# A fused attention and mixer kernel: conversions spread over the steps, v as two float16 parts, weight loads queued behind transposes, six scale factors in one product

## The chip, the cores and the metric

The program runs on one core of a Trainium2 chip. The core has TensorE (matmuls, PE in the profile), VectorE (DVE), ScalarE (ACT), GpSimd (POOL) and SyncE (SP, which issues the DMAs). The metric is device time in microseconds, the median over the executions that were timed.

## The reference

Causal attention with 4 batches, 12 heads, 448 positions and a head size of 64, then a token and channel mixer, then a layer in which a learned angle rotates the values:

```python
scores = q @ k.T / 8;  scores[mask] = -1e9;  attn = softmax(scores);  x = attn @ v      # 48 heads
h  = relu(x.T @ w_tok1) @ w_tok2;  u = x + h.T                  # over the positions
x2 = u + relu(u @ w_ch1) @ w_ch2                                # over 768 channels
th = x2 @ w_theta;  y = w_tok_r @ (x2*cos(th)) + w_tok_i @ (x2*sin(th));  u = x2 + y
out = u + relu(u @ w_ch)
```

The weights come as float64, q, k and v as float32.

## The kernel before

**Attention** runs over 24 pairs of heads (batch and pair of heads), each in 7 steps (the list `TILES`), so 168 steps, numbered through. A step takes one tile of scores: `scores` multiplies, reduces the row's maximum on VectorE (L338), takes the exponential on ScalarE (L340), and then hands the probabilities over in one of two ways. In pairs 0 to 11 (`NATPV`) TensorE transposes float32 probabilities (L347) and `pv` multiplies them with float32 v (L375). In pairs 12 to 23 the probabilities are split into two float16 parts `ph` (L157, L360), a transposing DMA on SP's queue makes `pt` of them (L363), and `pv` multiplies with v cut into three bfloat16 parts (L386): `prep` makes those parts with two subtractions on VectorE (L164, `v_mid`). `pv` of a step comes 4 steps (`LAG`) after its scores. `finish` divides by the row sums, and after each second pair `tokmix` does the first mixer.

**Units.** The channel mixer is 96 units of 18 matmuls of 128x448: for each batch and each half `fh`, 6 of `ch1_unit` (relu on ScalarE L459, float16 high part on POOL L160, low part on VectorE L461) and 6 of `ch2_unit` (its result is scaled with a factor `f` and added on VectorE, L473). `f` is one small product on POOL (L130) per unit. A unit's weights are float16 pairs `ws`, 384 KB, which `load_unit` streams from DRAM on SP's queue (L222). `UNIT_STEPS` says at which step each unit starts; the units that are left when attention ends run in a dense row, and behind them comes the third layer (from L657).

**Conversions.** The 24 tiles of `w_ch1` and `w_ch2` and four of `w_tok` are first made float32 from float64 in steps of their own: a load of 768 KB into `raw`, `abs64` on ScalarE (L173), three operations on VectorE (L180 to L182), squares on ScalarE (L124), a small matmul with `power`, which chooses a power of two `s`, then the high part on POOL (L160) and the low part on VectorE (L193, `ws`), and a store. The table `ROUNDINGS` sets their steps, one about every 3.4 steps from 14 to 92. Six tiles of `w_ch` are converted late.

**Before a batch's units**, `split_ready` calls `power` for the scale `s_u` and splits the six tiles `accs` into `ut` (high part ScalarE L157, low part VectorE L193). In `power` the products on POOL are `s` and `p`.

**Order.** A scheduler builds each engine's queue from the order of the code and priorities (`tc.high_priority`); `tc.issue_after(x)` puts what its block issues behind x on x's engine. Every engine and SP's queue take their instructions in order, so a waiting one holds those behind it. On-chip buffers are shared by tag: 8 of `ws`, 5 of `pt`, 4 of `f`, 3 of `ph` and `raw`, 4 PSUM banks for `ps_mm`.

Of the kernel before, what the change touches and what calls it, by code (L numbers as in the profile page):

```python
# [35 lines left out]
FIRST_UNIT, DENSE, RATE = 50, 88, (42, 29)  # L36
UNIT_STEPS = [FIRST_UNIT + n * (DENSE - FIRST_UNIT) // 14 if n < 14 else
              DENSE + -(-(n - 14) * RATE[0] // RATE[1]) for n in range(72)]
ROUNDINGS = [(at_step, n - 4) for n, at_step in enumerate((3, 4, 8, 9))] + [(14 + n * 78 // 23, n) for n in range(24)]
# [15 lines left out]
def fused(ctx, tc, q, k, v, w_tok1, w_tok2, w_ch1, w_ch2, w_theta, w_tok, w_ch, out):  # L55
# [76 lines left out]
    def power(p, s, sq):  # L132

        ps = mm_bank()
        n = sq.shape[-1]
        nc.tensor.matmul(ps[:, 0:1], lhsT=ones, rhs=tiny, start=True, stop=False)
        for j in range(n):
            nc.tensor.matmul(ps[:, 0:1], lhsT=ones, rhs=sq[:, j:j + 1], start=False, stop=j == n - 1)
        g = main.tile([P, 2], F32, tag="g", name="g", bufs=4)
        nc.vector.tensor_scalar(out=g[:, 0:1].bitcast(U32), in0=ps[:, 0:1].bitcast(U32), scalar1=1, scalar2=EXPONENT,  # L140
                                op0=ALU.logical_shift_right, op1=ALU.bitwise_and)
        two_over(g[:, 1:2], g[:, 0:1])
        product(s, g[:, 1:2], 2.0 ** -51, 1.0)
        product(p, g[:, 0:1], 2.0 ** 64, 1.0)
# [122 lines left out]
    def prep(b, pr):  # L267
# [28 lines left out]
        v1 = vr.bitcast(BF16).rearrange("p (n w) -> p n w", w=2)[:, :, 1]  # L296
        vm = ap2.tile([P, 9 * D], F32, tag="v_mid", name="v_mid", bufs=1)
        rest_to(pick("v"), vm, vr, v1)
        v2, v3 = (vm.bitcast(BF16).rearrange("p (n w) -> p n w", w=2)[:, :, z] for z in (1, 0))
        rest_to(pick("v"), v3, vm, v2)  # L300
        return qs, kh, kl, (v1, v2, v3)
# [3 lines left out]
    class Pair:  # L305
        def __init__(self, b, pr, parts):
            self.b, self.pr = b, pr
            self.qs, self.kh, self.kl, self.v = parts
# [57 lines left out]
    def pv(pp, i, h):  # L366
# [11 lines left out]
        if i == 0:  # L378
            jobs = [(0, c, 8) for c in range(3)] + [(1, c, 8) for c in range(2)]
        else:  # L380
            jobs = [(0, c, 6 + h) for c in range(3)]
            for u in range(i):
                jobs += [(1 + u, c, 2 * u + h) for c in range(3)]
                jobs += [(1 + i + u, c, 2 * u + h) for c in range(2)]
# [4 lines left out]
    def finish(pp, xb, xg):  # L389
        ps, sm = pp.ps, pp.sm  # L390
        nc.vector.tensor_scalar(out=sm[:, 0:7], in0=sm[:, 0:7], scalar1=1e-9, scalar2=1.0 if pp.native_pv else PSC, op0=ALU.add, op1=ALU.mult)
# [48 lines left out]
    ready = set()  # L440

# [25 lines left out]
    def ch2_unit(b, uT, acc, fh, d, w):  # L467
        ps = mm_bank()
        f = main.tile([P, 1], F32, tag="f", name="f", bufs=4)
        product(f, p_w2[:, fh * 6 + d:fh * 6 + d + 1], h_scale[0], 1.0)  # L470
# [15 lines left out]

    def load_unit(n):
        if n < len(units) and n not in loaded and (n >= 24 or n in stored):
            b, fh, c, t = units[n]
            loaded[n] = stream_tile(wd[f"c{c}", fh, t])  # L490
# [4 lines left out]
    def split_ready():  # L495

        b = halves[0]
        if b < B and None not in accs[b]:
            s = s_u[:, b:b + 1]
            power(p_u[:, b:b + 1], s, sq_u[b])  # L500
# [49 lines left out]
    def run_units(n):  # L550
        for _ in range(n):
# [11 lines left out]
            for ahead in range(LOOK + (u >= 24)):  # L563
                load_unit(at[0] + ahead)
# [35 lines left out]
    for n, (b, pr, t) in enumerate(steps):  # L600
        if t == 0:
            eng.update(ENGINES.get(b * NPR + pr, {}))
# [40 lines left out]
        run_units(sum(at_step == n for at_step in UNIT_STEPS))  # L643
    for n in range(len(steps) - LAG, len(steps)):
# [308 lines left out]
```

## Time and profile before

| | us |
|---|---|
| median of 3 runs | 905.37 (903.42 to 909.47) |
| profiled execution, its own time | 907.62 |
| its span, first to last instruction | 905.8 |
| busy: TensorE, VectorE, ScalarE, POOL | 868.4, 632.0, 538.1, 166.0 |
| granted TensorE clock, mean | 0.981 |

The span is 1.8 us shorter than the execution's own time. A busy TensorE is counted from modelled ends of pipelined matmuls. Step 56's scores are reduced at 121.4 us, step 84's at 210.4, step 126's at 330.2, and the last one's at 478.

### The profile page before, as it was taken

How to read it: one execution, taken by the hardware profiler on the slowest of the kernel's cores; microseconds unless marked ns; L12 is line 12 of the kernel's file. 1: busy time of each engine (PE TensorE's matmuls, PEld its weight loads, DVE VectorE, ACT ScalarE, POOL GpSimd, SP SyncE). 2: the span in 40 equal slices, each digit the busy share in tenths (PEclk: the TensorE clock that was granted, in tenths of full speed). 3: DMA queues.
4: the chain of work that ended last, by engine and by line, in shares of the span. 5: the costliest groups of instructions: out<-in, count | busy, mean ns of one | idle time of the engine just before them, and what ended most of it. 6: DMA issues, size and time to landing. Idle time of an engine off the chain costs nothing.

```text
span 905.8 us, 16756 instructions
## 1 busy us (share of the span) xinstructions
PE 868.4 (96%) x5979; PEld 563.7 (62%) x5979; DVE 632.0 (70%) x1499; ACT 538.1 (59%) x1247; POOL 166.0 (18%) x313
## 2 busy tenths in 40 slices
PE   7999699998988999899999998999999999999998
PEld 6888567776755667565666564556555555555554
DVE  7899867979997776738686328767875557566442
ACT  6788766767765654546573328546755457566441
POOL 3142322314141110101211102052211001101000
PEclk9999989999899999999999999999999999999999
DMA  7867745767799986747448568740440231231011
GB/s 225 243 194 237 281 166 194 259 210 202 211 279 319 261 204 140 202 110 193 142 103 224 162 195 298 258 131 10 145 143 29 86 114 39 92 114 45 21 57 72
DMA packets 105795, 149.67 MB, mean 165 GB/s; under 512 B 61104, under 2 KB 72304, under 8 KB 105712
## 3 DMA queue, kind: packets, MB, share of 16 engines
q1 hardware_dynamic: 105168, 147.59, 54.4%
q0 software_dynamic: 384, 0.79, 0.4%
q8 instruction: 47, 0.77, 0.4%
q14 instruction: 36, 0.29, 0.1%
q10 hardware_dynamic: 160, 0.23, 0.1%
HBM read 112.39 MB, written 22.81 MB: 149 GB/s over the span
## 4 chain that ended last, share of the span: by engine, by line
PE 74%; DVE 10%; DMA 8%; ACT 3%; issue 3%; POOL 1%; SPq 1%; DVEq 0%; ACTq 0%; POOLq 0%
PE ps_mm L228 17%; PE ps_mm L227 17%; PE ps_mm L229 17%; DMA pt<-ph 4%; PE ps_sc L229 3%; PE ps_sc L227 3%; PE ps_sc L228 3%; PE ps_pv L375 3%; PE ps_sc L331 2%; PE ps_pv L386 2%; PE ps_mm L347 2%; DVE sb L338 1%; PE ps_sc L333 1%; DVE wf L181 1%; DMA ws<-w_c 1%
## 5 line engine op out<-in xcount | busy, mean ns | idle before, releaser
L227 PE MATMUL ps_mm<-h,ws 128*128 128x448 f16 x432 | 152.8, 356 | 2.8 <-DMA ws<-w_c 2.8
L228 PE MATMUL ps_mm<-h,ws 128*128 128x448 f16 x432 | 153.4, 356 | 0.0
L229 PE MATMUL ps_mm<-h,ws 128*128 128x448 f16 x432 | 153.2, 356 | 0.0
L227 PEld LDWEIGHTS <-ws 128*128 128x128 f16 x720 | 71.1, 99 | 70.0 <-issue 5.7
L227 PE MATMUL ps_mm<-ut,ws 128*128 128x448 f16 x288 | 103.2, 359 | 8.8 <-ACT ut L157 8.2
L229 PEld LDWEIGHTS <-ws 128*128 128x128 f16 x720 | 71.1, 99 | 65.1 <-issue 5.2
L228 PEld LDWEIGHTS <-ws 128*128 128x128 f16 x720 | 71.1, 99 | 62.1 <-issue 4.9
L340 ACT ACTIVATE sb<-sb,mx 128x320 f32<-128x320 f32 (+3 forms) x168 | 89.3, 533 | 26.8 <-DVE mx L338 22.6
L228 PE MATMUL ps_mm<-ut,ws 128*128 128x448 f16 x288 | 103.0, 358 | 0.3 <-DVE ut L193 0.3
L229 PE MATMUL ps_mm<-ut,ws 128*128 128x448 f16 x288 | 102.8, 357 | 0.0
L338 DVE CUSTOM_DVE_ANT_0 sb<-ps_sc,mask 128x320 f32<-128x320 f32 (+3 forms) x168 | 73.8, 454 | 13.2 <-PE ps_mm L347 8.8
L124 ACT ACTIVATE junk<-acc 128x448 bf16<-128x448 f32 x72 | 41.2, 572 | 61.6 <-DVE acc L845 40.7
L375 PE MATMUL ps_pv<-v_raw,ptf 128*128 128x128 f32 (+1 forms) x456 | 63.2, 276 | 1.9 <-DVE x L398 1.7
L375 PEld LDWEIGHTS ps_pv<-v_raw,ptf 128*128 128x128 f32 x456 | 58.8, 191 | 6.9 <-ACT sb L340 1.9
L459 ACT ACTIVATE t<-ps_mm,c_scale 128x448 f32<-128x448 f32 x48 | 30.0, 628 | 54.5 <-PE ps_mm L229 45.9
L160 POOL TENSOR_SCALAR h<-t 128x448 f16<-128x448 f32 x48 | 31.3, 653 | 150.6 <-ACT t L459 150.3
L461 DVE TENSOR_TENSOR h<-t,h 128x448 f16<-128x448 f32 x48 | 31.3, 654 | 37.6 <-POOL h L160 37.5
L360 DVE SCALAR_TENSOR_TENSOR ph<-sb,ph 128x64 f16<-128x64 f32 (+3 forms) x156 | 43.0, 321 | 16.4 <-ACT ph L157 16.1
L157 ACT ACTIVATE ph<-sb 128x192 f16<-128x192 f32 (+3 forms) x84 | 36.5, 442 | 29.3 <-DMA pt<-ph 28.5
L130 POOL TENSOR_SCALAR f<-p_w,c_h 128x1 f32<-128x1 f32 x48 | 24.6, 516 | 145.2 <-DVE acc L473 129.0
L473 DVE SCALAR_TENSOR_TENSOR acc<-ps_mm,f,acc 128x448 f32<-128x448 f32 x48 | 32.4, 678 | 25.1 <-PE ps_mm L229 24.9
L227 PE MATMUL ps_sc<-th,ut 128*128 128x384 f16 x144 | 46.9, 326 | 0.0
(210 smaller groups left out, 2118.4 us busy)
## 6 DMA issues: line engine op xcount, KB each, us to landing
ws<-w_c SPq DMA_DIRECT2D x120, 384.0 KB, 4.0
raw<-in_w_ch_dram SPq DMA_DIRECT2D x30, 768.0 KB, 4.5
w_c<-ws SPq DMA_DIRECT2D x30, 384.0 KB, 3.8
q_raw<-in_q_dram SPq DMA_DIRECT2D x16, 448.0 KB, 3.6
k_raw<-in_k_dram SPq DMA_DIRECT2D x16, 448.0 KB, 5.6
v_raw<-in_v_dram SPq DMA_DIRECT2D x24, 288.0 KB, 3.4
x2d<-acc SPq DMA_DIRECT2D x24, 224.0 KB, 3.2
acc<-x2d SPq DMA_DIRECT2D x24, 224.0 KB, 2.9
```

The source lines that it names most:

```text
L124: nc.scalar.activation(j[:, 0:src.shape[-1]], src, AF.Square, accum_out=dst)
L157: nc.scalar.activation(dst, src, AF.Copy, scale=scale)
L160: e.tensor_scalar(out=dst, in0=src, scalar1=scale, scalar2=0.0, op0=ALU.mult, op1=ALU.add)
L227: nc.tensor.matmul(ps, lhsT=ka(a[:, 0]), rhs=kb(b[:, 0]), start=first, stop=False)
L228: nc.tensor.matmul(ps, lhsT=ka(a[:, 0]), rhs=kb(b[:, 1]), start=False, stop=False)
L229: return nc.tensor.matmul(ps, lhsT=ka(a[:, 1]), rhs=kb(b[:, 0]), start=False, stop=last)
L338: pp.first = nc.vector.tensor_tensor_reduce(out=dst, in0=src, in1=msk, op0=ALU.add, op1=ALU.min, scale=-0.125, scalar=3.0e38, accum_out=pp ...
L340: pp.last = nc.scalar.activation(sb[:, 0:kk], sb[:, 0:kk], AF.Exp, bias=pp.mx[:, j:j + 1], scale=-1.0, accum_out=pp.sm[:, j:j + 1])
L360: nc.vector.scalar_tensor_tensor(out=dst, in0=sb[:, c0:c1], scalar=PSC, in1=hi[:, c0:c1], op0=ALU.mult, op1=ALU.subtract)
L375: pp.pv = nc.tensor.matmul(pp.ps[:, reg:reg + n], lhsT=pt[:, u], rhs=pp.v[0][:, vt * D:vt * D + n], start=(u == 0), stop=(u == len(blks) - 1))
L461: gates[0] = nc.vector.tensor_tensor(out=t[:, 1], in0=f, in1=t[:, 0], op=ALU.subtract)
L473: nc.vector.scalar_tensor_tensor(out=acc[d], in0=ps[:, 0:S], scalar=f, in1=acc[d], op0=ALU.mult, op1=ALU.add)
```

## The change

Five things change. (1) `ROUNDINGS`: conversions stand 5 steps apart up to step 49, then 3.2 apart from 52 to 100. (2) `UNIT_STEPS`: the first unit starts at step 52 instead of 50, the first 12 stand 3 steps apart, 12 more 1.75 apart from step 88, and the dense rate of 29 units in 42 steps starts at 107 with the 24th. By the table 28 units have started by step 107 before, and 24 now. (3) v of pairs 12 to 23 is scaled by a power of two and cut into two float16 parts, `v_hi` on POOL (`copy_to("P", ...)`) and the rest on VectorE, written into `v_raw`; `pv` makes three products of each block of probabilities (high with both parts, low with the high one) instead of five. ScalarE squares v, and a small matmul and POOL's products `sv` choose the scale. (4) `load_unit` issues its DMA behind the latest transposing DMA of the current pair (`behind`), and always one unit further ahead. (5) From batch 1 on the six factors `f` of a half are one product `f6` of 128x6. `power` for `s_u` gets a high priority.

```diff
-FIRST_UNIT, DENSE, RATE = 50, 88, (42, 29)
-UNIT_STEPS = [FIRST_UNIT + n * (DENSE - FIRST_UNIT) // 14 if n < 14 else
-              DENSE + -(-(n - 14) * RATE[0] // RATE[1]) for n in range(72)]
-ROUNDINGS = [(at_step, n - 4) for n, at_step in enumerate((3, 4, 8, 9))] + [(14 + n * 78 // 23, n) for n in range(24)]
+FIRST_UNIT, DENSE, RATE = 52, 107, (42, 29)
+UNIT_STEPS = [FIRST_UNIT + 3 * n if n < 12 else 88 + (n - 12) * 7 // 4 if n < 24 else
+              DENSE + -(-(n - 23) * RATE[0] // RATE[1]) for n in range(72)]
+ROUNDINGS = [(at_step, n - 4) for n, at_step in enumerate((3, 4, 8, 9))]
+ROUNDINGS += [(14 + 5 * n if n < 8 else 52 + (n - 8) * 16 // 5, n) for n in range(24)]
...
-    def power(p, s, sq):
+    def power(p, s, sq, unit=None):
...
-        product(p, g[:, 0:1], 2.0 ** 64, 1.0)
+        if p is not None:
+            product(p, g[:, 0:1], 2.0 ** 64, 1.0)
+        if unit is not None:
+            product(unit, g[:, 1:2], 2.0 ** -51, PSC)
...
-        v1 = vr.bitcast(BF16).rearrange("p (n w) -> p n w", w=2)[:, :, 1]
-        vm = ap2.tile([P, 9 * D], F32, tag="v_mid", name="v_mid", bufs=1)
-        rest_to(pick("v"), vm, vr, v1)
-        v2, v3 = (vm.bitcast(BF16).rearrange("p (n w) -> p n w", w=2)[:, :, z] for z in (1, 0))
-        rest_to(pick("v"), v3, vm, v2)
-        return qs, kh, kl, (v1, v2, v3)
+        return qs, kh, kl, (vr,)
+
+    values = {}
+
+    def value_squares(n):
+        sq = main.tile([P, 1], BF16, tag="sqv", name="sqv", bufs=2)
+        squares(sq, parts[n][3][0])
+        values[n] = sq
+
+    def value_split(n):
+
+        vr = parts[n][3][0]
+        sc = main.tile([P, 2], F32, tag="sv", name="sv", bufs=3)
+        scale, unit = sc[:, 0:1], sc[:, 1:2]
+        power(None, scale, values.pop(n), unit)
+        hi = ap2.tile([P, 9 * D], F16, tag="v_hi", name="v_hi", bufs=2)
+        copy_to("P", hi, vr, scale)
+        lo = vr.bitcast(F16).rearrange("p (n w) -> p n w", w=2)[:, :, 0]
+        nc.vector.scalar_tensor_tensor(out=lo, in0=vr, scalar=scale, in1=hi, op0=ALU.mult, op1=ALU.subtract)
+        parts[n] = (*parts[n][:3], (hi, lo), unit)
...
-            jobs = [(0, c, 8) for c in range(3)] + [(1, c, 8) for c in range(2)]
+            jobs = [(0, 0, 8), (0, 1, 8), (1, 0, 8)]
         else:
-            jobs = [(0, c, 6 + h) for c in range(3)]
+            jobs = [(0, 0, 6 + h), (0, 1, 6 + h)]
             for u in range(i):
-                jobs += [(1 + u, c, 2 * u + h) for c in range(3)]
-                jobs += [(1 + i + u, c, 2 * u + h) for c in range(2)]
+                jobs += [(1 + u, 0, 2 * u + h), (1 + u, 1, 2 * u + h), (1 + i + u, 0, 2 * u + h)]
...
-        f = main.tile([P, 1], F32, tag="f", name="f", bufs=4)
-        product(f, p_w2[:, fh * 6 + d:fh * 6 + d + 1], h_scale[0], 1.0)
+        if b == 0:
+            f = main.tile([P, 1], F32, tag="f", name="f", bufs=4)
+            product(f, p_w2[:, fh * 6 + d:fh * 6 + d + 1], h_scale[0], 1.0)
+        else:
+            if d == 0:
+                f_six[0] = main.tile([P, DT], F32, tag="f6", name="f6", bufs=2)
+                product(f_six[0], p_w2[:, fh * 6:fh * 6 + 6], h_scale[0], 1.0)
+            f = f_six[0][:, d:d + 1]
...
+    behind = [ExitStack]
+
     def load_unit(n):
         if n < len(units) and n not in loaded and (n >= 24 or n in stored):
             b, fh, c, t = units[n]
-            loaded[n] = stream_tile(wd[f"c{c}", fh, t])
+            with behind[0]():
+                loaded[n] = stream_tile(wd[f"c{c}", fh, t])
...
-            power(p_u[:, b:b + 1], s, sq_u[b])
+            with tc.high_priority(AHEAD):
+                power(p_u[:, b:b + 1], s, sq_u[b])
...
-            for ahead in range(LOOK + (u >= 24)):
+            for ahead in range(LOOK + 1):
...
+        behind[0] = lambda pp=(b, pr): queued(pairs[pp])
...
+        nx = b * NPR + pr + 1
+        nxt = (nx // NPR, nx % NPR)
+        split_next = nx < B * NPR and nx not in NATPV
+        if t == 2 and split_next:
+            with tc.issue_after(pairs[b, pr].last.ins):
+                value_squares(nxt)
         if n >= LAG:
             with tc.high_priority(AHEAD):
                 late_step(n - LAG)
+            if t == 4 and split_next:
+                with tc.issue_after(pairs[steps[n - LAG][0:2]].pv.ins), tc.high_priority(AHEAD // 2):
+                    value_split(nxt)
```

The names at three places. On POOL, where the first units begin (`p_u` and `s_u` are `split_ready`'s products, `c_h` and `f` the units' factors, `ws` and `s` a conversion's), the queue before:

```order
L130 TENSOR_SCALAR p_u_148<-g_1407 128x1
L130 TENSOR_SCALAR c_h_1487<-p_fh_147,p_u_148 128x1
L130 TENSOR_SCALAR f_2083<-p_w2_143,c_h_1487 128x1
L130 TENSOR_SCALAR f_2169<-p_w2_143,c_h_1487 128x1
L130 TENSOR_SCALAR f_2249<-p_w2_143,c_h_1487 128x1
L130 TENSOR_SCALAR f_2408<-p_w2_143,c_h_1487 128x1
L130 TENSOR_SCALAR s_u_149<-g_1407 128x1
L130 TENSOR_SCALAR p_w2_143<-g_1476 128x1
L130 TENSOR_SCALAR s_1472<-g_1476 128x1
L160 TENSOR_SCALAR ws_1471<-wf_1364,s_1472 128x768
```

and the same place now:

```order
L131 TENSOR_SCALAR p_u_148<-g_1326 128x1
L131 TENSOR_SCALAR c_h_1456<-p_fh_147,p_u_148 128x1
L131 TENSOR_SCALAR f_2107<-p_w2_143,c_h_1456 128x1
L131 TENSOR_SCALAR s_u_149<-g_1326 128x1
L131 TENSOR_SCALAR p_w2_143<-g_1445 128x1
L131 TENSOR_SCALAR f_2203<-p_w2_143,c_h_1456 128x1
L131 TENSOR_SCALAR s_1441<-g_1445 128x1
L164 TENSOR_SCALAR ws_1440<-wf_1364,s_1441 128x768
```

`s_u`, for which the split of the first units' input waits, stood behind four products `f` and stands behind one.

On SP, from pair 14 to pair 15 (`ws` loads are a unit's weights, `w_c...<-ws` a conversion's store, `DMA_TRANSPOSE` the probabilities), the queue before:

```order
L363 DMA_TRANSPOSE pt<-ph 128x7x128
L363 DMA_TRANSPOSE pt<-ph 128x2x128
L363 DMA_TRANSPOSE pt<-ph 128x3x128
L476 DMA x2d_2_71<-acc 128x448
L222 DMA ws<-w_c_1_5_116 128x1536
L222 DMA ws<-w_c_0_0_93 128x1536
L222 DMA ws<-w_c_0_1_94 128x1536
L222 DMA ws<-w_c_0_2_95 128x1536
L476 DMA x2d_3_72<-acc 128x448
L222 DMA ws<-w_c_0_3_96 128x1536
L222 DMA ws<-w_c_0_4_97 128x1536
L222 DMA ws<-w_c_0_5_98 128x1536
```

and, at the transposes of the same sizes, now:

```order
L382 DMA_TRANSPOSE pt<-ph 128x7x128
L501 DMA x2d_0_69<-acc 128x448
L501 DMA x2d_1_70<-acc 128x448
L382 DMA_TRANSPOSE pt<-ph 128x2x128
L226 DMA ws<-w_c_1_3_114 128x1536
L382 DMA_TRANSPOSE pt<-ph 128x3x128 x2
L174 DMA raw<-in_w_ch_dram 128x1536
L287 DMA v_raw<-in_v_dram 128x576
L565 DMA w_c_1_4_115<-ws 128x1536
L382 DMA_TRANSPOSE pt<-ph 128x5x128 x2
L283 DMA q_raw<-in_q_dram 128x896
L226 DMA ws<-w_c_1_4_115 128x1536
```

Seven loads of weights stood between two transposes, with a store of `acc` among them; now there is one such load between two groups of transposes, and a load of `raw` beside it.

On POOL, about pair 18 (`sv` are v's scale and its counterpart, `h2` the high part of a `ch1_unit`'s result `t`), the queue before:

```order
L160 TENSOR_SCALAR h2_4797<-t_4796 128x448
L160 TENSOR_SCALAR h2_4864<-t_4863 128x448
L160 TENSOR_SCALAR h2_4943<-t_4942 128x448
L130 TENSOR_SCALAR f_5339<-p_w2_143,c_h_4575 128x1
L130 TENSOR_SCALAR f_5404<-p_w2_143,c_h_4575 128x1
L130 TENSOR_SCALAR p_u_148<-g_5167 128x1
L130 TENSOR_SCALAR c_h_5466<-p_fh_147,p_u_148 128x1
L130 TENSOR_SCALAR c_h_6394<-p_fh_147,p_u_148 128x1
L130 TENSOR_SCALAR s_u_149<-g_5167 128x1
```

and now:

```order
L131 TENSOR_SCALAR sv_4515<-g_4519 128x1 x2
L164 TENSOR_SCALAR v_hi_4524<-v_raw_4342,sv_4515 128x576
L164 TENSOR_SCALAR h2_4658<-t_4657 128x448
L164 TENSOR_SCALAR h2_4728<-t_4727 128x448
L131 TENSOR_SCALAR sv_4869<-g_4873 128x1 x2
L164 TENSOR_SCALAR h2_4783<-t_4782 128x448
L164 TENSOR_SCALAR v_hi_4878<-v_raw_4619,sv_4869 128x576
L131 TENSOR_SCALAR p_u_148<-g_4947 128x1
L131 TENSOR_SCALAR c_h_5585<-p_fh_147,p_u_148 128x1
```

The v copies are new here; the second `v_hi` stands behind an `h2` that waits for a unit's `t`, and the single products `f` are gone.

## Rows read from the trace of the kernel before

**Rows 1.** The page: busy time of each engine, its share and instructions.

```profile
PE 868.4 (96%) x5979; PEld 563.7 (62%) x5979; DVE 632.0 (70%) x1499; ACT 538.1 (59%) x1247; POOL 166.0 (18%) x313
```

**Rows 2.** Windows: stretch, length; PE, PEld, DVE, ACT, POOL busy (instructions); granted clock, DMA share, GB/s.

```profile
0.00:25.00 25.00, 19.96 (x125) 16.87 (x126) 18.48 (x63) 17.84 (x50) 7.24 (x19) 1.00 0.77 238
25.00:100.00 75.00, 71.93 (x514) 62.56 (x511) 69.55 (x177) 60.50 (x166) 22.74 (x36) 1.00 0.72 228
100.00:121.40 21.40, 13.85 (x78) 9.30 (x77) 18.06 (x40) 16.71 (x38) 7.05 (x13) 0.76 0.76 273
121.40:210.40 89.00, 89.00 (x624) 68.92 (x623) 68.04 (x160) 58.88 (x144) 24.82 (x35) 1.00 0.58 200
210.40:330.20 119.80, 109.52 (x947) 75.41 (x946) 101.83 (x282) 78.92 (x201) 26.81 (x40) 0.93 0.92 249
330.20:450.00 119.80, 115.59 (x924) 74.49 (x922) 77.44 (x211) 61.98 (x153) 16.51 (x32) 0.97 0.66 167
450.00:550.00 100.00, 97.25 (x777) 62.24 (x776) 55.15 (x139) 45.96 (x110) 13.24 (x35) 1.00 0.61 176
550.00:905.80 355.80, 351.33 (x2005) 193.91 (x2003) 223.47 (x435) 197.34 (x392) 47.57 (x103) 1.00 0.31 100
```

**Rows 3.** Windows of line 338 alone, two instructions a step: DVE busy (instructions).

```profile
0.00:121.40 121.40, 25.09 (x112) 0.96 0.74 238
121.40:210.40 89.00, 12.91 (x57) 1.00 0.58 200
210.40:330.20 119.80, 18.30 (x85) 0.93 0.92 249
```

**Rows 4.** Groups by form, products with v: busy, mean ns, idle before.

```profile
L386 PE MATMUL ps_pv<-v_raw,pt 128*128 128x64 bf16 x384 | 36.3, 194 | 9.8 <-DMA pt<-ph 7.8 <-issue 2.0
L386 PEld LDWEIGHTS <-pt 128*128 128x128 f16 x996 | 35.0, 98 | 16.5 <-DMA pt<-ph 8.9 <-issue 3.5
```

**Rows 5.** The chain in order of time: start, length, what.

```profile
310.26 1.06 PE ps_pv L386 x36
...
866.81 0.57 PE ps_mm L229 x3
```

**Rows 6.** Groups by form, VectorE: conversion and v.

```profile
L181 DVE SCALAR_TENSOR_TENSOR wf<-raw,wf 128x768 uint32<-128x768 uint32 x30 | 31.4, 1047 | 0.3
...
L193 DVE SCALAR_TENSOR_TENSOR ws<-wf,s,ws 128x768 f16<-128x768 f32 x30 | 30.8, 1025 | 9.5 <-POOL ws L160 6.3 <-ACT ws L157 3.1
...
L182 DVE SCALAR_TENSOR_TENSOR wf<-raw,wf 128x768 uint32<-128x768 uint32 x30 | 29.1, 970 | 0.1
...
L180 DVE TENSOR_SCALAR wf<-wf 128x768 uint32<-128x768 uint32 x30 | 20.4, 678 | 2.7 <-ACT wf L173 2.6
...
L164 DVE TENSOR_TENSOR v_mid<-v_mid 128x576 bf16<-128x576 f32 x12 | 9.9, 824 | 0.0
...
L164 DVE TENSOR_TENSOR v_mid<-v_raw 128x576 f32<-128x576 f32 x12 | 9.0, 752 | 0.7 <-PE ps_pv L386 0.5
```

**Rows 7.** Timeline of POOL before the first unit: start, length, what.

```profile
111.26 2.40 POOL L130 TENSOR_SCALAR f<-p_w,c_h 128x1 f32<-128x1 f32 x4
113.64 0.18 POOL L130 TENSOR_SCALAR s_u<-g 128x1 f32<-128x1 f32 x1
...
114.22 0.91 POOL L160 TENSOR_SCALAR ws<-wf,s 128x768 f16<-128x768 f32 x1
```

**Rows 8.** Timeline of PE: the first unit's first matmul, idle before it, releaser.

```profile
114.57 0.53 PE L227 MATMUL ps_mm<-ut,ws 128*128 128x448 f16 x1 [5.61 <-ACT ut L157]
```

**Rows 9.** Tile `pt`, all 84 transposing DMAs: issue to landing.

```profile
DMA to landing us min/median/max: 2.3/3.3/9.1
```

**Rows 10.** Waits: who for whom, us in total, times, longest.

```profile
POOL h L160 <- ACT t L459: 150.3, 38, 20.1
```

**Rows 11.** Timeline at 253 us, POOL beside VectorE.

```profile
252.99 1.36 POOL L160 TENSOR_SCALAR ws<-wf,s 128x768 f16<-128x768 f32 x1
253.58 1.58 DVE L181 SCALAR_TENSOR_TENSOR wf<-raw,wf 128x768 uint32<-128x768 uint32 x1
```

More of the change, by code (lines that the diff above doesn't have):

```diff
@@ L307, in __init__ @@
             self.b, self.pr = b, pr
-            self.qs, self.kh, self.kl, self.v = parts
+            self.qs, self.kh, self.kl, self.v = parts[:4]
+            self.unit = parts[4] if len(parts) > 4 else 1.0
             self.mx = ap2.tile([P, 7], F32, tag="mx", name="mx")
@@ L390, in finish @@
         ps, sm = pp.ps, pp.sm
-        nc.vector.tensor_scalar(out=sm[:, 0:7], in0=sm[:, 0:7], scalar1=1e-9, scalar2=1.0 if pp.native_pv else PSC, op0=ALU.add, op1=ALU.mult)
+        nc.vector.tensor_scalar(out=sm[:, 0:7], in0=sm[:, 0:7], scalar1=1e-9, scalar2=pp.unit, op0=ALU.add, op1=ALU.mult)
         nc.vector.reciprocal(out=sm[:, 0:7], in_=sm[:, 0:7])
@@ L440, in fused @@
     ready = set()
+    f_six = [None]
     def domain(b, fh):
@@ L643, in fused @@
         run_units(sum(at_step == n for at_step in UNIT_STEPS))
+    behind[0] = ExitStack
     for n in range(len(steps) - LAG, len(steps)):
```

## Prediction

> **What bounds the kernel now.** I read the page first: TensorE is busy 868.4 of 905.8 us [rows 1], so 37.4 us are idle. Then the windows by stretch [rows 2], for where that is and how fast the clock ran: the granted clock is short by 5.1 us in 100 to 121 (0.24 of 21.4), 8.4 in 210 to 330 and 3.6 in 330 to 450, which with 37.4 is about 54 us that TensorE could at most win back without less work. 5.0 of it are the start and 4.5 the end [rows 2], which nothing here touches. The reader is to see four stretches, which I cut at steps 56, 84 and 126 (112, 57 and 85 instructions of line 338, two a step [rows 3]):
>
> - 0 to 121.4 us: VectorE leads. It is busy 69.55 of 75 us between 25 and 100; from 100 on TensorE stands for 7.5 us and runs at a granted clock of 0.76 [rows 2].
> - 121.4 to 210.4: TensorE is busy all 89.0 us; VectorE has 21 us to spare [rows 2].
> - 210.4 to 330.2: VectorE 101.8 of 119.8, DMA 0.92 busy, TensorE idle 10.3 us [rows 2].
> - from 330.2: TensorE sets the time nearly everywhere; 4.2 and 2.75 us idle up to 550 [rows 2].
>
> So a microsecond of TensorE work counts in the second and fourth stretch, one of VectorE work in the first and third.
>
> **The products with v.** A pair had 83 matmuls (5, and twice 8, 13, 18) and has 51 (3, and twice 5, 8, 11): 32 fewer, 384 in 12 pairs. The chain shows 36 of them in 1.06 us [rows 5], 29.4 ns each, so 11.3 us in all; their 194 ns [rows 4] is latency that overlaps. Each weight load lasts 98 ns [rows 4], more than three such pitches, and hides beside the matmuls. The Trainium skill, TensorE: Matmul & The Clock Gate, section "LDWEIGHTS (loading the stationary operand)", gives a load of 128 columns about 107 ns; if loads set the pitch, 384 of them would be worth 41 us. The chain disagrees with that use of it, since 36 loads would then need 3.9 us, so I give it no chance. Twelve times two small matmuls for v's scale are bounded by 0.03 us each (the same pitch), 0.7 us. Half of the 11.3, the six pairs 12 to 17, lies in the third stretch, where TensorE has idle time: it counts nothing by itself. The other half, 5.6 us, counts.
>
> **Conversions and the first unit (0 to 121.4).** In VectorE's order 9 conversions begin between steps 14 and 56 where 13 did. One is 1.047 + 0.970 + 0.678 + 1.025 = 3.7 us [rows 6], so VectorE loses 14.9 us. TensorE's own work is unchanged, and between 25 and 100 it is visibly idle for 3.1 us only [rows 2]; I take -3 there. Then comes the first unit. Its matmul waited 5.61 us for `ut` [rows 8], and `ut` for `s_u`, which POOL issued behind four `f` of 2.40 us together [rows 7]. Three of them stand behind it now: 3 x 0.60 = 1.8 us. Together with fewer conversions in front of the splits on VectorE, and with the clock that the stop cost (5.1 us), I take -8 of the 12.6. Sum -11. If only the three `f` count it is -2; if TensorE loses no time after its start, -16.
>
> **121.4 to 210.4.** TensorE is full. In its order 11.0 units stand before step 84's scores, 9.9 now, and VectorE gets a conversion more and four of the six low parts of `ut`, with 21 us to spare [rows 2]. The missing unit is 18 matmuls of 0.57/3 = 0.19 us [rows 5], -3.7 us of work; against it, the first unit's wait can now fall here. I take -1, from -4 to +4.
>
> **210.4 to 330.2.** Here the conversions come back: VectorE's order has 9 from step 84 to 126, and had 6, +11.2 us. For v it had 0.752 + 0.824 = 1.58 us a pair [rows 6]; the new remainder is bounded by 0.75 (its own width, one subtraction) and 1.03 (768 columns, the same operation) [rows 6]. I take 0.85 and 0.3 for two one-column operations, so -0.4 a pair, -2.6 in six. Net +8.6 on 101.8 us. VectorE can then not be done before 110.4, which is -9; at the 93% of 25 to 100 it needs 118.7, which is -1; if its 18 us of idle time here stay, +8.6. These 18 us come with bunched DMAs: a transposing DMA lands in 2.3 to 9.1 us [rows 9], and the new order of SP has one load of weights between two groups of transposes where it had seven. So I take -1.
>
> **From 330.2 on.** TensorE's order has 26.0 units before step 126's scores and had 28.8: 2.8 x 3.4 = +9.5 us that move behind it. The products give -5.6. Of the idle 6.95 us and the 3.6 us of clock up to 550 [rows 2], transposes ahead of the loads and four more units in front of the third layer's loads should save some; I take -5, between 0 (the DMA engines are as full as before, so the new order gives nothing) and -10. Sum -1, from -6 to +4.
>
> **What costs nothing.** POOL's 12 copies for v_hi are bounded by 0.91 us each (768 columns [rows 7]), its 36 fewer `f` give more back, and it is busy 166 of 905.8 us [rows 1]. That cover is gone where a copy stands behind a waiting instruction (third rival). Squares of v, one ScalarE operation per pair, lie on an engine that is busy 79 of 119.8 us there [rows 2]. `unit` in `finish` replaces a constant. A POOL copy may also stretch VectorE: at 253 us the two overlap, and an operation with two inputs takes 1.58 us [rows 11] where the mean is 1.047 [rows 6]. The Trainium skill, GPSIMD Engine Reference, section "1. Specifications", says that POOL shares its way into SBUF with VectorE instructions of two SBUF inputs. By these rows twelve copies could cost 12 x 0.53 = 6.4 us if each met such an operation; the 48 `h` and 24 `ws` copies of before are in the means already, so I add nothing and leave it within the bounds.
>
> **Sum.** -11 - 1 - 1 - 1 = -14 on the profiled 907.6, so 893.6; the median of the runs lies 2.25 lower, and so does the forecast: 891.
>
> **The rivals.** (1) *The gain is only lent*: VectorE pays the full +8.6 in the third stretch, because its waits there stay. Sum -11 - 1 + 8.6 - 1 = -4.4: 901. For it: the stretch is VectorE's already, and the conversions return to it. Against it: the loads are spread. (2) *Everything flows*: -16 - 3 - 7 - 6 = -32: 873. For it: three of four stretches lose time by waits that the new orders shorten. Against it: VectorE would have to be busy 98% of the third one. (3) *Slower*: VectorE's remainder of v waits for `v_hi`, and POOL has, as in the order about pair 19, an `h2` in front of it, which waits for a unit's relu. Such waits are 150.3 us in 38 times, 4.0 each [rows 10]. If VectorE stands 4.0 us at each of 12 splits and nothing hides half of it, 891 + 24 to 48, about 919 at 28. It decides against the change from 2.0 us at each split. Against it: only some splits have an `h2` there, and POOL's copies are ordered by readiness. (4) *It does not do what it says*: transposes land no sooner. Then the last stretch is +4 and the third about +4: 901, with the first rival.
>
> **How the numbers follow.** A measurement of this kernel can tell about 1%, 9 us, from no change. The forecast (883 to 898) gets 0.46, rivals 1 and 4 together 0.24, rival 2 0.19, rival 3 0.11. Faster by over 1% is below 896.3: 0.46 x 0.87 + 0.19 + 0.24 x 0.1 = 0.61. Slower by over 1%, above 914.4: 0.11 x 0.7 = 0.08, with 0.01 for a broken first stretch 0.09. The same: 0.30. The range 874 to 907 leaves out half of rival 2 and nearly all of rival 3, about 2 in 10.
>
> **What would show it.** In the changed profile step 56 should stand near 110 us with VectorE less busy before it; the first unit's wait should be near 3 us; between step 84 and 126 VectorE should be busy above 90%, and TensorE more idle than 10.3 us; matmuls of the products with v should count 612, still 29 ns apart; the landing of transposes should have a lower maximum. Wrong would make it: VectorE idle at the v remainder, a third stretch longer than 125 us, or a new stop where `s_u` of batch 1 waits behind an `h2`.

## Result: slower by half a per cent

The changed kernel's time is 909.11 us (median of 12 executions, 906.89 to 911.58) against 904.11 for the kernel before (12, 901.43 to 909.47): a ratio of 1.0054, 95% interval 1.0037 to 1.0071. The forecast was 891, from 874 to 907. The profiled span went from 905.8 to 909.2 us.

The page of the changed kernel, busy time of each engine (before: [rows 1]):

```profile
PE 858.4 (94%) x5619; PEld 552.2 (61%) x5619; DVE 629.9 (69%) x1511; ACT 543.4 (60%) x1271; POOL 170.0 (19%) x319
```

TensorE has 360 matmuls fewer and 10 us less to do, and is idle 50.8 us where it was 37.4. The windows say where; first those cut as in [rows 2], then those cut at the changed kernel's own steps 56, 84 and 126 (113.8, 199.0 and 335.4 us):

```profile
25.00:100.00 75.00, 72.76 (x526) 64.32 (x525) 57.27 (x164) 57.47 (x161) 16.52 (x27) 1.00 0.58 188
100.00:121.40 21.40, 19.14 (x128) 15.37 (x127) 20.97 (x51) 20.04 (x50) 9.58 (x12) 0.92 0.75 263
121.40:210.40 89.00, 87.33 (x607) 67.22 (x605) 76.30 (x185) 63.46 (x159) 27.46 (x45) 1.00 0.67 231
210.40:330.20 119.80, 91.89 (x707) 59.87 (x706) 99.50 (x265) 75.59 (x191) 32.44 (x51) 0.90 0.94 251
330.20:450.00 119.80, 117.67 (x856) 75.81 (x853) 83.69 (x233) 72.63 (x185) 17.63 (x38) 1.00 0.67 167
450.00:550.00 100.00, 96.05 (x676) 58.72 (x675) 56.67 (x140) 43.33 (x98) 15.13 (x34) 0.98 0.59 174
```

```profile
113.80:199.00 85.20, 83.53 (x583) 65.06 (x583) 73.56 (x165) 62.82 (x155) 25.39 (x36) 1.00 0.68 237
199.00:335.40 136.40, 108.49 (x810) 70.79 (x809) 111.70 (x307) 85.86 (x219) 37.41 (x63) 0.91 0.92 248
```

Before step 56 the change does what it was to do: VectorE is busy 57.3 us from 25 to 100 where it was 69.6, and the stop at 109 us with its low clock (0.76) has nearly gone. From step 84 to 126 it goes wrong: 136.4 us where it took 119.8, with TensorE idle 27.9 us at a clock of 0.91.

A mark by steps alone deceives here, because the units' table has moved as well. So the next windows count one line of a unit's matmuls (L231, L227 before; six of them are one unit) between the same steps; of the kernel before, then of the changed one. Columns: stretch, length, PE and PEld busy (instructions), clock, DMA share, GB/s.

```profile
0.00:121.40 121.40, 7.64 (x18) 3.10 (x18) 0.96 0.74 238
121.40:210.40 89.00, 27.13 (x76) 8.16 (x76) 1.00 0.58 200
210.40:330.20 119.80, 40.83 (x112) 12.01 (x113) 0.93 0.92 249
```

```profile
0.00:113.80 113.80, 5.04 (x13) 2.42 (x13) 0.99 0.63 202
113.80:199.00 85.20, 24.05 (x67) 7.29 (x67) 1.00 0.68 237
199.00:335.40 136.40, 41.88 (x114) 12.17 (x114) 0.91 0.92 248
```

At 3.4 us a unit (18 matmuls of 0.19, [rows 5]): the first stretch is 7.6 us shorter but holds 0.8 units less, 4.8 us net; the second 3.8 shorter with 1.5 units less, so 1.3 longer net; the third is 16.6 longer with 0.3 units more, 15.6 net; the rest 1.8 shorter, although 2.0 units have been pushed into it, 8.6 net. The sum is +3.5, and the spans differ by 3.4.

The waits of TensorE in the changed kernel: who for whom, us in total, times, longest.

```profile
PE ps_mm L231 <- DMA ws<-w_c: 11.6, 3, 4.2
PE ps_sc L350 <- DVE mx L357: 8.9, 7, 5.0
...
PE ps_pv L404 <- DMA pt<-ph: 5.4, 6, 1.7
```

TensorE's wait for weights, the first line, was 2.8 us in one wait before. Two of the three now lie in the third stretch. The chain shows the first of them:

```profile
269.33 7.86 DMA pt<-ph
...
280.62 7.70 DMA w_c<-ws
288.38 3.76 DMA ws<-w_c
292.19 0.56 PE ps_mm L231
```

A freshly converted tile is stored, which takes 7.7 us here; the load of the same tile is issued as soon as the store has landed, takes 3.8 more, and only then the unit can begin. SP's queue has such a pair a second time, store at 303.24 and load at 309.73:

```profile
280.62 0.37 SPq L565 DMA_DIRECT2D w_c<-ws  x1
...
288.38 0.33 SPq L226 DMA_DIRECT2D ws<-w_c  x1
...
303.24 0.38 SPq L565 DMA_DIRECT2D w_c<-ws  x1
...
304.72 4.92 SPq L382 DMA_TRANSPOSE pt<-ph  x3
309.73 2.44 SPq L226 DMA_DIRECT2D ws<-w_c  x5
```

Here the store had landed at 309.09, and the load went out 0.6 us later, behind three transposing DMAs that stood before it in the queue; the chain goes over these and not over the store. The longest stop of the stretch is not for weights at all, but for a row's maximum (`mx`):

```profile
307.33 0.55 PE L350 MATMUL ps_sc<-kh,qs 128*128 128x256 f32 x1 [4.99 <-DVE mx L357]
```

From 302.4 until that maximum VectorE was busy without a gap, with a division, two operations of a conversion and the splits of `ph` and `xg`.

By the changed table the last conversion is at step 100, its store at 105 and its unit at 107, 2 steps of slack; before, the last was at 92, stored at 97 for a unit at 102. The third wait, 3.5 us up to 485.8 ("at 482" below), is another case: five loads of weights stood there behind the last transposing DMA.

### The profile page after: what moved, and what is told of

Same layout as the page of the kernel before. It is cut to its first block, busy times and chain, and to the rows that moved or that the text cites. A ratio compares the mean times of both kernels' runs of the same rounds, so it can differ in the third digit from the quotient of the medians.

```text
span 909.2 us, 16049 instructions
## 1 busy us (share of the span) xinstructions
PE 858.4 (94%) x5619; PEld 552.2 (61%) x5619; DVE 629.9 (69%) x1511; ACT 543.4 (60%) x1271; POOL 170.0 (19%) x319
## 4 chain that ended last, share of the span: by engine, by line
PE 68%; DMA 10%; DVE 10%; ACT 7%; issue 3%; SPq 1%; POOL 1%; ACTq 0%; DVEq 0%; POOLq 0%
PE ps_mm L231 15%; PE ps_mm L233 15%; PE ps_mm L232 15%; DMA pt<-ph 4%; PE ps_sc L350 4%; PE ps_pv L394 4%; PE ps_sc L231 3%; PE ps_sc L232 3%; PE ps_sc L233 3%; DMA ws<-w_c 3%; PE ps_mm L366 2%; ACT sb L359 2%; DMA q_raw<-in_q_dram 1%; DVE ph L379 1%; ACT junk L125 1%
## 5 line engine op out<-in xcount | busy, mean ns | idle before, releaser
L231 PE MATMUL ps_mm<-h,ws 128*128 128x448 f16 x432 | 153.3, 357 | 11.6 <-DMA ws<-w_c 11.6
L231 PEld LDWEIGHTS <-ws 128*128 128x128 f16 x720 | 70.7, 98 | 74.7 <-DMA ws<-w_c 12.3
L231 PE MATMUL ps_mm<-ut,ws 128*128 128x448 f16 x288 | 101.8, 354 | 0.8 <-DVE g L141 0.6
L232 PE MATMUL ps_mm<-ut,ws 128*128 128x448 f16 x288 | 101.6, 353 | 0.0
L233 PE MATMUL ps_mm<-ut,ws 128*128 128x448 f16 x288 | 101.6, 353 | 0.0
L379 DVE SCALAR_TENSOR_TENSOR ph<-sb,ph 128x64 f16<-128x64 f32 (+3 forms) x156 | 45.4, 334 | 32.0 <-ACT ph L161 31.2
L350 PE MATMUL ps_sc<-kh,qs 128*128 128x256 f32 (+2 forms) x112 | 46.4, 418 | 8.3 <-DVE mx L357 8.2
L231 PE MATMUL ps_sc<-th,ut 128*128 128x384 f16 x144 | 46.9, 326 | 0.0
L233 PE MATMUL ps_sc<-th,ut 128*128 128x384 f16 x144 | 46.8, 326 | 0.0
```

The source lines that it names most:

```text
L231: nc.tensor.matmul(ps, lhsT=ka(a[:, 0]), rhs=kb(b[:, 0]), start=first, stop=False)
L232: nc.tensor.matmul(ps, lhsT=ka(a[:, 0]), rhs=kb(b[:, 1]), start=False, stop=False)
L233: return nc.tensor.matmul(ps, lhsT=ka(a[:, 1]), rhs=kb(b[:, 0]), start=False, stop=last)
L350: nc.tensor.matmul(ps[:, 0:n], lhsT=lhs, rhs=cut(pp.kh), start=True, stop=pp.kl is None)
L379: nc.vector.scalar_tensor_tensor(out=dst, in0=sb[:, c0:c1], scalar=PSC, in1=hi[:, c0:c1], op0=ALU.mult, op1=ALU.subtract)
```

## Experiments

All times are compared with runs of the kernel before on the same chip. The medians of before were 906.45 us for the first four runs, 905.73, 905.18 and 904.76 for the next three groups.

### First: which half costs

**Loads without the wait.** The rest as in the changed kernel.

```diff
-            with behind[0]():
-                loaded[n] = stream_tile(wd[f"c{c}", fh, t])
+            loaded[n] = stream_tile(wd[f"c{c}", fh, t])
```

> The changed kernel, but a unit's weights are loaded wherever the scheduler puts them and not behind the transposing DMA. Its profile has three waits of TensorE for weights, 4.1 us at 288, 4.5 at 309 and 3.6 at 482, 11.6 us in all. Theory 'late conversions' (the last conversions stand so near to the units that use them that their store lands after TensorE asks for the weights): the waits at 288 and 309 stay, only the one at 482, where five loads stood behind the last transpose, goes: about 905. Theory 'loads held behind transposes': all three go, with the clock that they cost: 896 or less. Theory 'VectorE' (the returned conversions simply add their 8.6 us to a stretch that VectorE bounds): no change, 909.

905.42 us, ratio 0.9987 (0.9969 to 1.0005). The wait at 482 us is gone; the two others remain, 8.4 us together, and step 126 is at 334.8 us, as late as with the wait. So the wait of the loads costs 0.7% here, but the third stretch is not its doing. That is what "late conversions" expected.

**The old conversions**, the new units.

```diff
-ROUNDINGS += [(14 + 5 * n if n < 8 else 52 + (n - 8) * 16 // 5, n) for n in range(24)]
+ROUNDINGS += [(14 + n * 78 // 23, n) for n in range(24)]
```

> The changed kernel with the old table of conversions (3.4 steps apart from 14 to 92), but the new table of units. The last conversion stands at step 92 and its unit at 107, 15 steps apart, where the change has 7. Late conversions: the waits at 288 and 309 go, the third stretch loses 10 us or more and the first gets back some 5 of its 7.6: about 902. Loads held behind transposes: the waits stay, 909 to 914. VectorE: the third stretch loses 8 to 11, the first gets back 7: 905 to 909, without any wait for weights having decided it.

902.99 us, 0.9963 (0.9948 to 0.9979). One wait for weights of 3.9 us is left, at 475 us and so outside the third stretch, which takes 128.1 us, with 105.1 us of VectorE work where the changed kernel has 111.7. The time is that of "late conversions"; the 8.3 us that the stretch loses fit "VectorE" as well.

**Both old tables**; v, the loads' wait, the six factors and the priority stay. The edit is the one above and

```diff
-FIRST_UNIT, DENSE, RATE = 52, 107, (42, 29)
+FIRST_UNIT, DENSE, RATE = 50, 88, (42, 29)
...
-UNIT_STEPS = [FIRST_UNIT + 3 * n if n < 12 else 88 + (n - 12) * 7 // 4 if n < 24 else
-              DENSE + -(-(n - 23) * RATE[0] // RATE[1]) for n in range(72)]
+UNIT_STEPS = [FIRST_UNIT + n * (DENSE - FIRST_UNIT) // 14 if n < 14 else
+              DENSE + -(-(n - 14) * RATE[0] // RATE[1]) for n in range(72)]
```

> The changed kernel with both old tables, of conversions and of units; what is left is v in two parts, loads behind transposes, the sixfold factor and the priority. Late conversions: 904.1 less the 5 to 11 us of the products with v, less 1.8 for three factors at the first unit: 893 to 898. Loads held behind transposes: a wait for weights of 4 us or more remains, 900 to 905. VectorE: 893 to 898 as well, with VectorE's share in the third stretch as before.

895.73 us, 0.9886 (0.9860 to 0.9913): faster than both kernels. Two of the three theories had this range, so it does not tell them apart.

**The new tables alone**, put into the kernel before.

> The kernel before with both new tables alone. Late conversions: TensorE waits for weights between 280 and 320 us although nothing stands behind transposes, the third stretch is 15 us longer and the first 8 shorter: about 913. Loads held behind transposes: no such wait, 896 to 900 (the first stretch's gain alone). VectorE: the third stretch longer by 8.6 to 12 with VectorE above 90% busy: 905 to 908.

924.26 us, 1.0185 (1.0150 to 1.0220). The executions spread: the profiled one took 915.6, the five others 921.4 to 926.4, and the trace is of the first. None of the three expectations had this. In the trace one wait for weights of 3.2 us stands at 318 us, and the third stretch is only 2.1 us longer than before (121.9), but holds 84 matmuls of the units' line where it held 112, 4.7 units less: the loss is work pushed behind it. The two tables therefore cost 1.7% to 1.9%, and everything else together gains 1.1%.

### Second: what gains, and why the tables cost

**Both old tables, and loads without the wait.**

> The old tables for conversions and units, weight loads issued without the wait for a transposing DMA; the split of v, the six factors in one product and the priority stay. With the new tables, taking the wait of the loads away was worth 0.7% (909.1 against 905.4 us), a third of it a wait of TensorE of 3.6 us at 482 us where five loads stood behind the last transposing DMA. Theory (the wait of the loads costs whatever the tables): 0.982 to 0.984 of the kernel before, against 0.989 of the version with it, and the stop at 482 gone. Rival (with the old tables, whose loads come in bunches of seven, the wait does what it is for, and transposes land sooner): 0.989 or more, and TensorE's wait for pt longer than the 2 to 8 us of before.

894.36 us, 0.9862 (0.9838 to 0.9886), 0.24% better than with the wait, between theory and rival and within what the intervals leave open. TensorE waits 2.8 us for `pt` where it waited 4.4 with the wait.

**The late conversions earlier**: the changed kernel with one number changed.

```diff
-ROUNDINGS += [(14 + 5 * n if n < 8 else 52 + (n - 8) * 16 // 5, n) for n in range(24)]
+ROUNDINGS += [(14 + 5 * n if n < 8 else 52 + (n - 8) * 8 // 3, n) for n in range(24)]
```

> The changed kernel with one number changed: the conversions from step 52 on stand 2.67 steps apart instead of 3.2, so the last is at step 92 instead of 100, and its store 10 steps ahead of its unit instead of 2; those ahead of step 52, the units and all else stay. Theory (the third stretch is lost because the last conversions' stores land only when their units are due): the two waits for ws at 288 and 309 us go, the stretch from step 84 to 126 falls from 136.4 to 120 to 128 us, the first stretch keeps its gain (step 56 at 112 to 116), and the time is 0.990 to 0.996 of the kernel before. Rival (the conversions' work itself, VectorE's 3.7 us each and 1.1 MB of DMA each, is too much wherever it stands after step 56): the loss moves to the stretch from 56 to 84, and the time stays within 0.3% of the changed kernel's 1.005.

897.98 us, 0.9911 (0.9891 to 0.9932): the theory's time, and nearly its steps. Step 56 is at 111.6 us, and of the waits for weights one of 1.0 us is left in the third stretch, which takes 127.5:

```profile
196.60:324.10 127.50, 113.44 (x835) 75.54 (x834) 109.92 (x296) 84.84 (x215) 34.24 (x57) 0.93 0.92 244
```

**Six factors alone**, with the priority, in the kernel before.

```diff
+            with tc.high_priority(AHEAD):
+                power(p_u[:, b:b + 1], s, sq_u[b])
...
+            if d == 0:
+                f_six[0] = main.tile([P, DT], F32, tag="f6", name="f6", bufs=2)
+                product(f_six[0], p_w2[:, fh * 6:fh * 6 + 6], h_scale[0], 1.0)
+            f = f_six[0][:, d:d + 1]
```

> The kernel before with two edits alone: six factors f in one product from batch 1 on, and the priority of the products for s_u. Theory (the stall of the first unit is the queue of f in front of s_u on POOL): the wait of 5.6 us at 114 us falls to 2 to 4, step 56 1.5 to 4 us earlier, the time 0.996 to 0.998. Rival (the first unit waits for VectorE's conversions and their splits): step 56 unchanged within 1 us, the time 0.999 to 1.001.

905.68 us, 0.9994 (0.9976 to 1.0012), step 56 at 121.5: nothing. But the run does not test the queue in front of the first unit, as I had meant it to: batch 0 keeps single factors, and four `f` still stood ahead of `s_u`:

```profile
111.59 1.47 POOL L130 TENSOR_SCALAR f<-p_w,c_h 128x1 f32<-128x1 f32 x4
113.02 0.19 POOL L130 TENSOR_SCALAR s_u<-g 128x1 f32<-128x1 f32 x1
```

In the changed kernel one `f` stands there (108.39 to 109.42), because its units stand further apart; `s_u` comes at 109.44, 4.2 us earlier than in [rows 7].

**v alone**, in the kernel before.

```diff
-            jobs = [(0, c, 8) for c in range(3)] + [(1, c, 8) for c in range(2)]
+            jobs = [(0, 0, 8), (0, 1, 8), (1, 0, 8)]
```

(with the new split and the other two lines of the diff's `pv`).

> The kernel before with v in two float16 parts alone. 384 matmuls less at 29.4 ns are 11.3 us; half lies in the third stretch, where TensorE was idle for 10.3 us. Theory (half counts, with 2.6 us of VectorE): 0.991 to 0.994. Rival 1 (all of the 11.3 us counts): 0.986 to 0.989. Rival 2 (the remainder of v waits for its high part on POOL behind an h2, and takes back what the products give): 0.997 or more, with VectorE idle at the v remainder for more than 10 us in all.

894.38 us, 0.9879 (0.9857 to 0.9901): 11 us, rival 1. All of the 384 matmuls count, and this part alone is worth as much as the best of the above.

### Third: slack, amount, and the price of a matmul

**Old units, early conversions**: old `UNIT_STEPS`, the 2.67 steps of above, loads without the wait, v, six factors.

> The conversions 5 steps apart up to step 49 and 2.67 apart from 52 to 92, with the old table of units; v in two parts, six factors in one product, the priority; weight loads without the wait. Theory (the even spacing ahead of step 56 does win there, 5 to 7 us net, and its price later came only from the last conversions): 0.978 to 0.983 of the kernel before. Rival (a conversion costs VectorE and the DMA engines the same wherever it stands, so what the first stretch wins the later ones lose): 0.985 to 0.989, the same as with both old tables (0.986).

889.87 us, 0.9833 (0.9809 to 0.9858), at the theory's edge: against 0.9862 with the old conversions, the even spacing is worth some 0.3%, which the intervals do not quite tell from nothing.

**The last six earlier**, the others as changed.

```diff
-ROUNDINGS += [(14 + 5 * n if n < 8 else 52 + (n - 8) * 16 // 5, n) for n in range(24)]
+ROUNDINGS += [(14 + 5 * n if n < 8 else 52 + (n - 8) * 16 // 5 if n < 18 else 84 + (n - 18) * 8 // 5, n) for n in range(24)]
```

> The changed kernel with its last six conversions alone earlier: at steps 84, 85, 87, 88, 90 and 92 instead of 84 to 100; as many conversions begin after step 84 as in the changed kernel, only the slack between a store and its unit is larger. Theory (slack is what was missing): the waits for ws at 288 and 309 us go, the stretch from step 84 to 126 falls by 8 us or more from 136.4, the time is 0.989 to 0.996. Rival (six conversions after step 84 are too many for VectorE and the DMA engines, and the run with 2.67 steps had only four there): the waits turn into others, the time 1.002 or more.

904.44 us, 0.9992 (0.9975 to 1.0008), between the two: 0.6% better than the changed kernel, 0.8% worse than the run with 2.67 steps. The waits of TensorE from 200 to 335 us:

```profile
PE ps_sc L350 <- DVE mx L357: 9.3, 6, 2.4
PE ps_pv L404 <- DMA pt<-ph: 4.0, 6, 1.4
...
PE ps_mm L231 <- DMA ws<-w_c: 0.7, 2, 0.5
```

The waits for weights have gone from 8.1 us in this window to 0.7, as slack would have it. What remains is VectorE: its work in the third stretch is as large as in the changed kernel,

```profile
197.00:330.40 133.40, 110.79 (x824) 73.07 (x823) 114.03 (x306) 86.93 (x219) 36.88 (x64) 0.94 0.88 246
```

114.0 us against 109.9 with 2.67 steps, and TensorE waits for row maxima instead. So both were at work: too little slack, and too many conversions in this stretch.

**2.67 steps without the loads' wait.**

> The version with the conversions 2.67 steps apart, without the wait of the weight loads for a transposing DMA. Theory (the wait costs by itself, mostly after the last transposes at 480 us): 0.984 to 0.987, against 0.991 with it; TensorE's stop at about 470 us, when attention's last transposes are out, goes. Rival (the 0.7% that the wait cost in the changed kernel came from late stores that it delayed still more, and these are gone): 0.990 to 0.992.

897.36 us, 0.9919 (0.9899 to 0.9939), the same as with the wait: the rival. The stop at 471 us stays, 3.5 us where it was 3.3 with the wait, and five loads stand behind the last transposing DMA here too, so the wait of the loads is not what brings them there. Why it costs nothing in this pair no run shows.

**v with five products**: the new split, the old number of matmuls.

```diff
-                jobs += [(1 + u, 0, 2 * u + h), (1 + u, 1, 2 * u + h), (1 + i + u, 0, 2 * u + h)]
+                jobs += [(1 + u, c, 2 * u + h) for c in (0, 1, 1)] + [(1 + i + u, c, 2 * u + h) for c in (0, 1)]
```

> The kernel before with v in two float16 parts and five products of each block instead of three (two of the five repeat or add small terms, so that the output is slightly off). It keeps the new split of v and gives back the 384 matmuls. Theory (the gain of 1.2% is the matmuls): 0.997 to 1.003, so 9 to 13 us above the version with three products. Rival (the gain is VectorE's one operation less per pair, and the parts being ready earlier): 0.993 or less.

903.51 us, 0.9986 (0.9969 to 1.0004): the theory. The split by itself gains nothing that can be told; three products for five are worth 1.07%, 9.7 us, of the 11.3 that the pitch gives.

### Fourth: the units' table

**The dense row from step 86.** The first 12 units as changed, the rest at the old rate.

```diff
-UNIT_STEPS = [FIRST_UNIT + 3 * n if n < 12 else 88 + (n - 12) * 7 // 4 if n < 24 else
-              DENSE + -(-(n - 23) * RATE[0] // RATE[1]) for n in range(72)]
+UNIT_STEPS = [FIRST_UNIT + 3 * n if n < 12 else
+              86 + -(-(n - 12) * RATE[0] // RATE[1]) for n in range(72)]
```

> Conversions 2.67 steps apart from 52 to 92, loads without the wait, the first 12 units 3 steps apart from step 52 as in the changed kernel, but the dense row of units from step 86 on, at the old rate; 68 units have a step up to 167 by the table, against 64 in the changed one and 69 in the old one. Theory (the new units' table costs because its second part leaves TensorE without work in the stretch where VectorE sets the pace, and moves 4.6 units behind attention): 0.982 to 0.986, as with the old table (0.983). Rival (its first part costs: units that begin later around step 56): 0.990 or more, as with the new table (0.992).

886.74 us, 0.9803 (0.9780 to 0.9827): a little better than the theory, and the best version, though its interval overlaps that of the old units (0.9809 to 0.9858). It is 2.5% faster than the changed kernel. Its third stretch, all engines and then the units' line alone; after it the same two of the run that differs in the units' second part alone (0.9919):

```profile
196.70:330.30 133.60, 121.48 (x901) 79.19 (x899) 110.74 (x297) 85.01 (x217) 33.54 (x59) 0.96 0.95 254
...
196.70:330.30 133.60, 50.35 (x141) 14.61 (x141) 0.96 0.95 254
```

```profile
196.90:322.70 125.80, 112.53 (x839) 76.29 (x837) 107.58 (x291) 82.03 (x210) 34.76 (x56) 0.93 0.93 248
...
196.90:322.70 125.80, 41.73 (x117) 12.29 (x117) 0.93 0.93 248
```

It is 7.8 us longer and holds 4 units more, 13.6 us of TensorE work. In a stretch where VectorE sets the pace units go in part into TensorE's gaps, 7.8 us for four; left for later they cost their full 13.6. The stop of 3.5 us at 471 us is gone as well.

**The wait of the loads in the version with old units and early conversions.**

> The version with the old table of units and the conversions 5 and 2.67 steps apart (0.983), but with the weight loads behind the transposing DMA. Theory (the wait costs only where a load is late already, and here all stores are early): 0.982 to 0.986, no difference that can be told. Rival 1 (it costs by itself, as 0.989 against 0.986 with both old tables hinted): 0.987 to 0.990. Rival 2 (it wins, since transposes land sooner): 0.980 or less.

893.60 us, 0.9879 (0.9857 to 0.9901) against 0.9833: rival 1, though the intervals just touch. TensorE waits 5.8 us for `pt` with the wait and 3.1 without.

## Why the prediction was wrong

| part | shown by | worth |
|---|---|---|
| three products with v for five | v alone; five products | -1.2% (-1.1% the matmuls) |
| six factors, priority | alone | -0.06%, nothing |
| these with loads one unit further ahead | 0.9879 to 0.9862 | -0.2%, within the intervals |
| the new units' table | 0.9886 to 0.9963; 0.9833 to 0.9919 | +0.8%, +0.9% |
| of it the second part | 0.9803 to 0.9919 | +1.2% |
| the new conversions | 0.9963 to 1.0054 | +0.9% |
| the same, ending at 92 | 0.9963 to 0.9911 (new units); 0.9862 to 0.9833 (old) | -0.5%, -0.3% |
| the wait of the loads | four pairs | +0.7, +0.2, -0.1, +0.5% |

**The step that failed is the third stretch, -1.** The forecast of VectorE's work held: 110.4 us, and it was 111.7. What failed is "at the 93% of 25 to 100 it needs 118.7", on the ground that loads between transposes, once spread, would let VectorE's 18 us of waits shrink. VectorE was busy 82% of the third stretch (111.7 of 136.4), 85% before, and from 81% to 90% in all sixteen kernels that were traced; no order of loads brought it to 93%. In the trace the waits did not shrink: VectorE's idle time in the stretch went from 18.0 to 24.7 us. What VectorE and ScalarE waited for there (us in total, times, longest), before and then in the changed kernel:

```profile
DVE ph L360 <- ACT ph L157: 6.3, 9, 2.2
...
ACT ph L157 <- DMA pt<-ph: 10.5, 11, 1.7
```

```profile
DVE ph L379 <- ACT ph L161: 14.3, 7, 3.0
...
ACT ph L161 <- DMA pt<-ph: 21.0, 11, 3.8
```

VectorE's low part of `ph` waits for ScalarE's high part, and that waits until a transposing DMA has read an older `ph`. With the loads spread, both waits doubled; without the loads' wait the first was 14.1 us in the changed kernel, and in the three other pairs it was 1.6 to 4.6 us shorter without than with it.

At the 85% of before, 111.7 us of work make 131.4 us. The other 5 go with the two late stores, a mechanism that no rival had: I counted the conversions that the table moved, and not the steps between a conversion's store and its unit, which the two tables alone show. The run with the last six earlier bears this out: without these waits the share was 85% again (114.0 of 133.4). But a low share has other causes too: with the old conversions, where no unit of the stretch waits for weights, it was 82%. The first rival ("the gain is only lent") had the direction, at half the size of the 16.6 us.

**Where a conversion stands decides its price.** From step 56 to 84 TensorE is full and VectorE had 21 us to spare; the run with 2.67 steps does 77.4 us of VectorE work there where the changed kernel does 73.6, in the same 85 us. After step 84 the same conversion lengthens the stretch: the run with the last six earlier has 4.1 us more VectorE work there than the run with 2.67 steps (114.0, 109.9) and takes 5.9 us longer.

**The products with v** were sized at 29.4 ns, rightly: 612 are left, and 28 of them take 0.82 us in the chain, 29.3 each:

```profile
297.06 0.82 PE ps_pv L404 x28
```

The Trainium skill, TensorE: Matmul & The Clock Gate, section "Wait — 56ns, not 53.3ns?", gives a warm pitch of the moving columns at 2.4 GHz and some 2.5 ns more, by which 64 columns are estimated at 29.2 ns, and this trace agrees. The mis-sized term is that half of them counted nothing (-5.6). In the run with v alone TensorE's idle time in the third stretch stayed (11.1 us, before 10.3), but 2.3 units more were done there by the same table, and 4.2 more by step 167, with the step at the same time (477.4 us, before 478.0). Work that moves up took the freed place, so little of it was lost (9.7 of 11.3 us by the run with five products).

**The first stretch**, -11, brought 4.8 net of the units. The wait of 5.6 us did go, and the step was right in kind; the fewer conversions did the most of it. With the old conversions and the new units step 56 was at 118.9 us with 0.7 units less than before, 0.2 us net; with the new conversions and the old units it was at 118.4 with 0.3 units more, 4.1 net. The 12.6 us from which I took -8 counted some 2.1 twice: of the clock's 5.1 us these fell into the stop itself, when TensorE had nothing to do (109.0 to 114.6 us, granted clock 0.63). What `f` in front of `s_u` costs by itself no run here shows. **The second**, -1, and **the last**, -1, came out at -3.8 and -1.8 by their marks; the 2.8 units moved behind step 126 were 2.0. POOL's copies of v, bounded by 0.91 us each, took 0.95 in the mean; in the changed kernel nothing waited for them.

**Of the rivals**, the fourth was right on its one point: transposes land no sooner in the median (below). The third, a split of v that waits on POOL for an `h2`, did not happen: VectorE's remainder of v shows no idle time in front of it.

```profile
L318 DVE SCALAR_TENSOR_TENSOR v_raw<-v_raw,sv,v_hi 128x576 f16<-128x576 f32 x12 | 10.6, 886 | 0.0
```

Of what was to show it, the 612 products, TensorE's idle time and the lower maximum of the transposes' landing (7.9 us, before 9.1) came; step 56 stood at 113.8 and not near 110, and the first unit's wait was gone where 3 us were expected. VectorE above 90% from step 84 to 126 did not come, and "a third stretch longer than 125 us" did.

## What to carry to other kernels

Before moving preparatory work in time, look which engine sets the pace where it lands: here a conversion was free where TensorE was full and cost its whole length where VectorE led, and units were, in part, the other way round. For work handed on through DRAM count the steps from its store to its first use, and price a step by the DMA times at that place (here 7.7 + 3.8 us where the medians are 3.8 and 4.3). And when two tables move together, read progress as time less the work already done, not as the time of a step.

## What the runs showed of the hardware

Holding loads behind a transposing DMA did not make transposes land sooner in the median. Landing of all 84, in the changed kernel and in the same without the loads' wait:

```profile
DMA to landing us min/median/max: 2.3/3.4/7.9
```

```profile
DMA to landing us min/median/max: 2.3/3.6/7.7
```

The medians were 3.1 to 3.8 us in the fourteen other kernels, with and without the wait, and TensorE waited longer for `pt` with it in all four pairs: 5.4 us against 4.7, 4.4 against 2.8, 8.3 against 5.3, 5.8 against 3.1. Each is one trace, and two kernels that took the same time differ by as much as the smaller of these (7.8 before, 9.4 with six factors alone).

These stops of TensorE cost more than their length. The unit that had waited for its weights at 288 us:

```profile
292.19 0.56 PE L231 MATMUL ps_mm<-h,ws 128*128 128x448 f16 x1 [3.97 <-DMA ws<-w_c]
292.54 0.58 PE L232 MATMUL ps_mm<-h,ws 128*128 128x448 f16 x1
...
294.40 0.58 PE L231 MATMUL ps_mm<-h,ws 128*128 128x448 f16 x1
...
295.20 0.35 PE L231 MATMUL ps_mm<-h,ws 128*128 128x448 f16 x1
295.39 0.35 PE L232 MATMUL ps_mm<-h,ws 128*128 128x448 f16 x1
```

From 292.2 to 294.8 its matmuls start 0.37 us apart, later 0.19: 1.2 GHz and then 2.4. Seven steps of the slow pitch, 0.18 us more each, are 1.3 us on top of 4.0. After the stops between 301 and 313 us it was worse, with a granted clock of 0.50 for 17 us, in which TensorE was busy 7.85:

```profile
301.70:318.70 17.00, 7.85 (x34) 4.48 (x33) 11.69 (x37) 7.39 (x22) 1.06 (x3) 0.50 1.03 303
```
